# Scores of 32 left-over keys on four column tiles of the PE, spread by way of HBM, and the last chunk's sums behind its values

## The chip, the cores and the metric

One core of one Trainium2 chip. The metric is the device time of one execution in microseconds (us), median of several runs. PE is TensorE (its weight loads are shown as PEld), ACT is ScalarE, DVE is VectorE, POOL is GpSimd, SP is SyncE, which issues nearly all DMAs here.

## The reference, cut to what matters

```python
B, T, D = 2, 4000, 512
h = layernorm(x1)                                   # x1: after a first feed-forward block
q, k, v = h @ w_q, h @ w_k, h @ w_v
p = softmax(einsum('btd,bsd->bts', q, k) * D**-0.5)
x2 = x1 + einsum('bts,bsd->btd', p, v) @ w_o
# ... gated convolution with batch statistics, second feed-forward block, layernorm
```

Attention runs over 4000 keys for each of 2 x 4000 queries. Queries come in 16 chunks: 14 of 508 and 2 of 444 columns. 4000 keys are 31 tiles of 128 and 32 left over.

## The kernel before: the parts that matter

Weights are folded (`M` for queries and keys, `Wvo` for values and output), so keys and values are both `h`. For each key tile PE computes scores into a bank of PSUM, where its results land, ACT takes the exponential into a block `P`, DVE adds it to the running sums `acc`, and four steps later PE multiplies `P` with the keys' rows into four output banks.

```python
# attention, chunk g of W queries; KT = 32 key tiles, REST = 32, DC = 4, LAG = 4
for kt in range(KT):
    ps, b_ps = self.sbank()
    for cc in range(DC):                                # scores: 128 keys x W queries
        self.mm(ps[:, 0:W], self.hT[kc][:, kj, cc, :], self.qT[s][:, cc, 0:W], cc == 0, cc == DC - 1, ...)
    self.act(self.P[p][:, 0:W], ps[:, 0:W], AF.Exp, ...)
    n = REST if kt == KT - 1 else 128                   # of the last tile 32 rows count
    # DVE: acc[0:n] += P[0:n]
    if kt == KT - 1:
        self.split_sums(g)
    def values(...):                                    # four key tiles later
        for dc in range(DC):
            r = slice(dc*REST, (dc+1)*REST) if kt == KT - 1 else slice(0, 128)
            self.mm(self.Yb[dc][:, 0:W], self.h[kt][r, dc*128:(dc+1)*128], self.P[p][r, 0:W], ...,
                    **({"tile_position": (dc*REST, 0)} if kt == KT - 1 else {}))
```

The last key tile holds the same 32 keys four times, in rows 0-31, 32-63, 64-95 and 96-127. Its full-width scores are therefore four equal copies. The values use that: each of four row tiles of the PE takes one copy and makes a different quarter of the output, all at once. After the last chunk come the sums as matmuls of one column, then the last values:

```python
self.pop(3)                      # values of key tiles 28 to 30
self.sums_direct(last % 2)       # 8 matmuls with a column of ones, waits for split_sums
self.pop(1)                      # values of the left-over tile, then OT is copied out of PSUM
self.conv_b(tail, DC - 3)        # then the projections begin
```

## Time and profile before

| | before |
|---|---|
| time, median of 4 runs | 2040.98 us (2040.7 to 2041.0) |
| span of the profiled run | 2037.1 us |
| PE busy | 2028.9 us, 99% of the chain that ended last |
| one attention chunk of 508 queries | 68.32 us |
| scores of the left-over tile in it | 0.86 us |

How to read it: PE is full nearly throughout, so a change is worth what it takes off PE's stream, plus the few gaps at the seams between stages. Other engines only matter where they open such a gap.

### The profile page before, as it was taken

How to read it: one execution, taken by the hardware profiler on the slowest of the kernel's cores; microseconds unless marked ns; L12 is line 12 of the kernel's file. 1: busy time of each engine (PE TensorE's matmuls, PEld its weight loads, DVE VectorE, ACT ScalarE, POOL GpSimd, SP SyncE). 2: the span in 40 equal slices, each digit the busy share in tenths (PEclk: the TensorE clock that was granted, in tenths of full speed). 3: DMA queues.
4: the chain of work that ended last, by engine and by line, in shares of the span. 5: the costliest groups of instructions: out<-in, count | busy, mean ns of one | idle time of the engine just before them, and what ended most of it. 6: DMA issues, size and time to landing. Idle time of an engine off the chain costs nothing.

```text
span 2037.1 us, 24581 instructions
## 1 busy us (share of the span) xinstructions
PE 2028.9 (100%) x9682; PEld 1030.5 (51%) x9682; DVE 1081.5 (53%) x2187; ACT 743.7 (37%) x1277; POOL 107.6 (5%) x235
## 2 busy tenths in 40 slices
PE   9999999999999999999999999999999999999998
PEld 5555555554444444445444444444455555555555
DVE  4234443334556667666766676667674443434433
ACT  3433333333333333333333333333345443443433
POOL 1000000000000000000000000000011000000000
PEclk9999999999999999999999999999999999999999
DMA  8122245420101111114421111111143111111111
GB/s 189 49 62 62 54 102 124 96 70 19 16 16 27 25 32 26 27 26 94 106 57 23 26 29 32 24 27 26 44 135 93 32 32 42 32 32 42 29 34 38
DMA packets 253122, 104.43 MB, mean 51 GB/s; under 512 B 193412, under 2 KB 252487, under 8 KB 252999
## 3 DMA queue, kind: packets, MB, share of 16 engines
q1 hardware_dynamic: 252321, 102.44, 21.6%
q8 instruction: 78, 1.28, 0.3%
q14 instruction: 45, 0.37, 0.1%
q10 hardware_dynamic: 678, 0.34, 0.1%
HBM read 33.77 MB, written 23.34 MB: 28 GB/s over the span
## 4 chain that ended last, share of the span: by engine, by line
PE 99%; ACT 0%; DVE 0%; issue 0%; POOL 0%; DVEq 0%
PE s L512 56%; PE y L512 42%; ACT work L562 0%; DVE wff L1215 0%; PE y L540 0%; ACT keys L562 0%; POOL work L1224 0%; DVE work L559 0%; DVE work L876 0%; PE y L527 0%; DVE wff L1102 0%; DVE work L1222 0%; ACT xt L562 0%; DVE work L835 0%; DVE work L1229 0%
## 5 line engine op out<-in xcount | busy, mean ns | idle before, releaser
L562 ACT ACTIVATE work<-s 128x508 bf16<-128x508 f32 (+3 forms) x1060 | 621.7, 587 | 1211.5 <-PE s L512 1207.1
L512 PE MATMUL s<-work,wff 128*128 128x508 bf16 (+4 forms) x2640 | 628.3, 369 | 0.8 <-ACT work L562 0.4
L512 PE MATMUL s<-work,keys 128*128 128x508 bf16 (+1 forms) x2048 | 516.6, 374 | 0.1
L512 PE MATMUL y<-work,keys 128*128 128x508 bf16 (+2 forms) x2048 | 503.9, 373 | 0.0
L512 PE MATMUL y<-wff,work 128*127 128x512 bf16 (+1 forms) x2000 | 501.4, 378 | 0.0
L959 DVE TENSOR_TENSOR work<-work 128x508 f32<-128x508 f32 (+2 forms) x496 | 334.4, 674 | 281.6 <-ACT work L562 280.8
L512 PEld LDWEIGHTS s<-work,wff 128*128 128x128 bf16 x2640 | 252.6, 98 | 277.0 <-issue 4.7
L512 PEld LDWEIGHTS y<-wff,work 128*127 128x127 bf16 x2000 | 274.4, 137 | 170.9
L512 PEld LDWEIGHTS s<-work,keys 128*128 128x128 bf16 x2048 | 199.4, 98 | 232.0 <-DVE work L876 0.6
L512 PEld LDWEIGHTS y<-work,keys 128*128 128x128 bf16 (+1 forms) x2048 | 193.6, 97 | 233.1 <-issue 6.2
L758 DVE SCALAR_TENSOR_TENSOR xt<-y,xt 127x512 bf16<-127x512 f32 x125 | 77.7, 682 | 364.0 <-PE y L512 364.0
L512 PE MATMUL s<-work 128*127 128x512 bf16 (+4 forms) x775 | 196.9, 378 | 1.2 <-DVE work L1333 1.2
L624 DVE BATCH_NORM_STATS2 work<-xt 127x6 f32<-127x512 bf16 x311 | 195.2, 676 | 5.2 <-DMA xt<-in_x_dram 4.9
L631 POOL TENSOR_TENSOR work<-work 127x4 f32<-127x4 f32 (+1 forms) x76 | 76.5, 1007 | 1129.4 <-DVE work L629 1129.4
L512 PEld LDWEIGHTS s<-work 128*127 128x127 bf16 (+2 forms) x775 | 94.8, 124 | 75.6 <-issue 4.0
L644 DVE TENSOR_SCALAR work<-xt,work 127x512 bf16<-127x512 bf16 x309 | 111.4, 406 | 27.4 <-POOL work L631 23.2
L758 DVE SCALAR_TENSOR_TENSOR xt<-s,xt 127x512 bf16<-127x512 f32 x55 | 38.0, 691 | 148.7 <-PE s L512 148.7
L758 DVE SCALAR_TENSOR_TENSOR xt<-s,work,xt 127x512 bf16<-127x512 f32 x64 | 48.0, 750 | 30.9 <-PE s L512 30.3
L1113 DVE SCALAR_TENSOR_TENSOR wff<-wff,s 128x508 bf16<-128x508 f32 (+1 forms) x57 | 38.7, 678 | 41.5 <-PE s L512 41.3
L562 ACT ACTIVATE wff<-s 128x508 f32<-128x508 f32 (+1 forms) x67 | 39.5, 591 | 53.5 <-PE s L512 53.4
L562 ACT ACTIVATE work<-keys,work 128x508 bf16<-128x508 bf16 (+1 forms) x68 | 52.3, 774 | 0.4 <-DVE work L1229 0.2
L1194 POOL COPY wff<-wff 128x1 bf16<-128x1 bf16 x56 | 10.4, 187 | 637.8 <-DVE wff L1113 635.0
(92 smaller groups left out, 413.0 us busy)
## 6 DMA issues: line engine op xcount, KB each, us to landing
keys<-keysd SPq DMA_DIRECT2D x62, 128.0 KB, 2.3
keysd<-work SPq DMA_DIRECT2D x14, 448.0 KB, 3.2
out_dram<-work SPq DMA_DIRECT2D x14, 448.0 KB, 3.2
dcvd<-wff SPq DMA_DIRECT2D x48, 127.0 KB, 1.9
keys<-dcvd SPq DMA_DIRECT2D x12, 508.0 KB, 4.9
xt<-in_x_dram SPq DMA_DIRECT2D x13, 448.0 KB, 4.8
wff<-in_w_ff_a_dram SPq DMA_DIRECT2D x15, 256.0 KB, 5.2
work<-work SPq DMA_TRANSPOSE x208, 2.5
```

Source lines behind the costliest of these rows:

```text
L512: self.S.op("PE", lambda e: e.matmul(out, lhsT, rhs, start=start, stop=stop, **kw), reads=reads, writes=[bank], inc=stop if inc is None el ...
L562: return self.S.op("ACT", lambda e: e.activation(out, in_, func, **kw), reads=reads, writes=writes)
L624: self.S.op("DVE", lambda e: e.bn_stats(self.st[sl][:, ti, 0:6], x), reads=[b_x], writes=[self.b_st[sl][ti]])
L631: S.op("POOL", lambda e: e.tensor_tensor(out=self.rs[sl][:, 0:n], in0=self.mv[sl][:, 0:n, 1], in1=self.neghalf[0:TILE, 0:n], op=ALU.pow), ...
L644: self.S.op("DVE", lambda e: e.tensor_scalar(out, x, self.mv[sl][:, ti, 0:1], self.rs[sl][:, ti:ti + 1], ALU.subtract, ALU.mult), reads=[b ...
L758: self.S.op("DVE", lambda e: e.scalar_tensor_tensor(out=self.XT[g][rows], in0=ps[rows], scalar=scalar, in1=self.XT[g][rows], op0=ALU.mult, ...
L959: S.op("DVE", lambda e, p=p, n=n, acc=acc: e.tensor_tensor(out=acc, in0=acc, in1=self.P[p][0:n, 0:W], op=ALU.add), reads=[self.b_P[p], sel ...
L1113: self.S.op("DVE", lambda e: e.scalar_tensor_tensor(out=out, in0=th, scalar=1.0, in1=ps[:, 0:W], op0=ALU.add, op1=ALU.mult), reads=[b_ps, ...
L1194: S.op("POOL", lambda e: e.tensor_copy(self.G[gs][:, jj, 0:1], self.G[gp][:, jj, CHUNK:CHUNK + 1]), reads=[self.b_G[gp][jj]], writes=[self ...
```

## The change

Its intent: the scores of the 32 left-over keys are computed once and not four times. The 128 columns of the PE become four column tiles of 32; tile j holds the 32 keys and gets the j-th quarter of the queries, so 127 columns stream and not 508. The result then lies by quarters of the queries (rows 32j to 32j+31 hold quarter j), while the values want all queries in each of the four row groups. A store to HBM and four loads spread it. This happens at key tile 18, long before the values need it. Three smaller parts: at the start of attention matmuls of the feed-forward block move behind the last query group; in the last chunk the sums go behind the left-over values, with a block of the convolution behind the first projection; two PSUM copies go from ACT to DVE.

```diff
+    TAIL_AT = 18
+        self.pq = W.view(14336, 128); self.ptail = W.view(31744, CHUNK); self.pqd = nc.dram_tensor("pqd", [128, TILE], ...)
...
             for kt in range(KT):
+                if kt == self.TAIL_AT:
+                    self.tail_scores(g)
+                if kt < KT - 1:
                     (scores, exponential and sums of one key tile, as before)
...
-                        self.mm(self.Yb[dc][:, 0:W], self.h[kt][r, ...], self.P[p][r, 0:W], ...
+                        (the last tile reads self.ptail in place of self.P[p])
...
+    def tail_scores(self, g):
+        n = W // 4
+        parts = [(slice(j * REST, (j + 1) * REST), slice(j * n, (j + 1) * n)) for j in range(4)]
+        for cc in range(DC):
+            for j, (r, q) in enumerate(parts):
+                self.mm(ps[r, 0:n], hT[:, cc, r], self.qT[s][:, cc, q], cc == 0, cc == DC - 1, ...,
+                        inc=cc == DC - 1 and j == 3, tile_position=(0, j * REST))
+        self.act(self.pq[:, 0:n], ps[:, 0:n], AF.Exp, ...)
+        for r, q in parts:
+            (DVE: acc[s][r, q] += pq[r, 0:n])
+        self.store(self.pqd[:, 0:n], self.pq[:, 0:n], ...)
+        src = self.pqd[:, 0:n].rearrange("(j k) q -> k j q", j=4)
+        S.dma("SP", k, *[lambda e, r=r: e.dma_start(self.ptail[r, 0:W]..., src) for r, q in parts], ...)
...
         for dc in range(DC):
-            if dc == DC - 1:
-                self.pop(1)
             self.q_group(0, 0, dc)
+        self.pop(1)
...
         self.pop(3)
+        self.pop(1)
         self.sums_direct(last % 2)
-        self.pop(1)
-        self.conv_b(tail, DC - 3)
-        fill = [None, ...
+        fill = [lambda: self.conv_b(tail, DC - 3), ...
...
-        copy_away()
+        copy_away("DVE")
```

Left out: the load of the second batch's left-over keys moves from the 25th key tile of the second batch's first chunk to its 7th, since they are now needed at key tile 18.

More of the change, by code (lines that the diff above doesn't have):

```diff
@@ L359, in memory @@
         self.b_Wp2 = C.buf("Wp2", oWvo, 4096)
+        self.pq = W.view(14336, 128)
+        self.b_pq = W.buf("pq", 14336, 256)
+        self.ptail = W.view(31744, CHUNK)
+        self.b_ptail = W.buf("ptail", 31744, 2 * CHUNK)
+        self.pqd = nc.dram_tensor("pqd", [128, TILE], BF16, kind="Internal").ap()
+        self.b_pqd = Buf("pqd")
         GW = CHUNK + 4
@@ L942, in attention @@
                 kc, kj = divmod(kt, TPC)
-                ps, b_ps = self.sbank()
-                p = self.nxt("Pa", self.NP - 1) if self.any_score else self.nxt("P", self.NP)
-                for cc in range(DC):
-                    self.mm(ps[:, 0:W], self.hT[kc][:, kj, cc, :], self.qT[s][:, cc, 0:W],
-                            cc == 0, cc == DC - 1 and not self.any_score,
-                            [self.b_hT[kc][kj], self.b_qT[s][cc]], b_ps)
-                if self.any_score:
-                    self.mm(ps[:, 0:W], self.one3, self.m3[:, 0:W], False, True,
-                            [self.b_one3] + self.b_m3, b_ps)
@@ L952, in attention @@
-                self.act(self.P[p][:, 0:W], ps[:, 0:W], AF.Exp, [b_ps], [self.b_P[p]], scale=SCALE)
-                if kt == 0:
-                    S.op("DVE", lambda e, p=p: e.tensor_copy(self.acc[s][:, 0:W], self.P[p][:, 0:W]),
-                         reads=[self.b_P[p]], writes=[self.b_acc[s]])
-                else:
-                    n = REST if kt == KT - 1 else 128
-                    acc = self.acc[s][0:n, 0:W]
-                    S.op("DVE", lambda e, p=p, n=n, acc=acc: e.tensor_tensor(
-                        out=acc, in0=acc, in1=self.P[p][0:n, 0:W], op=ALU.add),
-                        reads=[self.b_P[p], self.b_acc[s]], writes=[self.b_acc[s]])
+                p = None
@@ new lines, in attention @@
+                if kt == self.TAIL_AT:
+                    self.tail_scores(g)
+                if kt < KT - 1:
+                    ps, b_ps = self.sbank()
+                    p = self.nxt("Pa", self.NP - 1) if self.any_score else self.nxt("P", self.NP)
+                    for cc in range(DC):
+                        self.mm(ps[:, 0:W], self.hT[kc][:, kj, cc, :], self.qT[s][:, cc, 0:W],
+                                cc == 0, cc == DC - 1 and not self.any_score,
+                                [self.b_hT[kc][kj], self.b_qT[s][cc]], b_ps)
+                    if self.any_score:
+                        self.mm(ps[:, 0:W], self.one3, self.m3[:, 0:W], False, True,
+                                [self.b_one3] + self.b_m3, b_ps)
+                    self.act(self.P[p][:, 0:W], ps[:, 0:W], AF.Exp, [b_ps], [self.b_P[p]], scale=SCALE)
+                    acc = self.acc[s][:, 0:W]
+                    if kt == 0:
+                        S.op("DVE", lambda e, p=p: e.tensor_copy(acc, self.P[p][:, 0:W]),
+                             reads=[self.b_P[p]], writes=[self.b_acc[s]])
+                    else:
+                        S.op("DVE", lambda e, p=p: e.tensor_tensor(out=acc, in0=acc, in1=self.P[p][:, 0:W], op=ALU.add),
+                             reads=[self.b_P[p], self.b_acc[s]], writes=[self.b_acc[s]])
@@ L969, in values @@
                     for dc in range(DC):
-                        r = slice(dc * REST, (dc + 1) * REST) if kt == KT - 1 else slice(0, 128)
-                        self.mm(self.Yb[dc][:, 0:W], self.h[kt][r, dc * 128:(dc + 1) * 128], self.P[p][r, 0:W],
-                                kt == 0, kt == KT - 1, [self.b_h[kt], self.b_P[p]], self.b_Y[dc],
-                                inc=kt == KT - 1 or dc == DC - 1,
-                                **({"tile_position": (dc * REST, 0)} if kt == KT - 1 else {}))
+                        r, x, b_x, at = slice(0, 128), self.P[p or 0], self.b_P[p or 0], {}
+                        if kt == KT - 1:
+                            r, x, b_x, at = slice(dc * REST, (dc + 1) * REST), self.ptail, self.b_ptail, {"tile_position": (dc * REST, 0)}
+                        self.mm(self.Yb[dc][:, 0:W], self.h[kt][r, dc * 128:(dc + 1) * 128], x[r, 0:W],
+                                kt == 0, kt == KT - 1, [self.b_h[kt], b_x], self.b_Y[dc],
+                                inc=kt == KT - 1 or dc == DC - 1, **at)
                     if kt == KT - 1:
@@ L994, in attention @@
                     for k in range(KT):
-                        if 6 + k * (2 * KT - 12) // KT == at:
+                        if (6 + k * (2 * KT - 12) // KT if k < KT - 1 else KT + 6) == at:
                             self.key_tile(1, k)
@@ L998, in attention @@
                 self.tick()
+    def tail_scores(self, g):
+        S, s, W = self.S, g % 2, width(g)
+        n = W // 4
+        ps, b_ps = self.sbank()
+        hT, b_hT = self.hT[TCB - 1][:, TPC - 1], self.b_hT[TCB - 1][TPC - 1]
+        parts = [(slice(j * REST, (j + 1) * REST), slice(j * n, (j + 1) * n)) for j in range(4)]
+        for cc in range(DC):
+            for j, (r, q) in enumerate(parts):
+                self.mm(ps[r, 0:n], hT[:, cc, r], self.qT[s][:, cc, q], cc == 0, cc == DC - 1 and not self.any_score,
+                        [b_hT, self.b_qT[s][cc]], b_ps, inc=cc == DC - 1 and j == 3, tile_position=(0, j * REST))
+        if self.any_score:
+            for j, (r, q) in enumerate(parts):
+                self.mm(ps[r, 0:n], self.one3[:, r], self.m3[:, q], False, True, [self.b_one3] + self.b_m3, b_ps,
+                        inc=j == 3, tile_position=(0, j * REST))
+        self.act(self.pq[:, 0:n], ps[:, 0:n], AF.Exp, [b_ps], [self.b_pq], scale=SCALE)
+        for r, q in parts:
+            acc = self.acc[s][r, q]
+            S.op("DVE", lambda e, acc=acc, r=r: e.tensor_tensor(out=acc, in0=acc, in1=self.pq[r, 0:n], op=ALU.add),
+                 reads=[self.b_pq, self.b_acc[s]], writes=[self.b_acc[s]])
+        self.store(self.pqd[:, 0:n], self.pq[:, 0:n], [self.b_pq], [self.b_pqd])
+        k = S.dsems[self.nxt("ld", 16)]
+        src = self.pqd[:, 0:n].rearrange("(j k) q -> k j q", j=4)
+        S.dma("SP", k, *[lambda e, r=r: e.dma_start(self.ptail[r, 0:W].rearrange("p (j q) -> p j q", j=4), src)
+                         for r, q in parts], reads=[self.b_pqd], writes=[self.b_ptail])
     def key_tile(self, b, kt):
@@ L1216, in depthwise @@
                                   reads=[b_ps], writes=[self.b_bst[cc]]),
-                lambda: self.act(self.dcv[t][cc][:, 0:W], ps[:, 0:W], AF.Copy, [b_ps], [self.b_dcv[t][cc]]))
+                lambda eng="ACT": self.away(eng, self.dcv[t][cc][:, 0:W], ps[:, 0:W], b_ps, [self.b_dcv[t][cc]]))
     def conv_scale(self, cc):
@@ L1404, in program @@
         for dc in range(DC):
-            if dc == DC - 1:
-                self.pop(1)
-                old -= 1
             self.q_group(0, 0, dc)
+        self.pop(1)
+        old -= 1
         tail = NCK - 2
@@ L1457, in gate @@
             gates.pop(0)(eng)
-        fill = [None, lambda: gates.append(self.conv_a(tail, DC - 3)), lambda: self.conv_b(tail, DC - 2),
+        fill = [lambda: self.conv_b(tail, DC - 3), lambda: gates.append(self.conv_a(tail, DC - 3)), lambda: self.conv_b(tail, DC - 2),
                 lambda: gates.append(self.conv_a(tail, DC - 2))]
@@ L1465, in prepare @@
                 gate("POOL")
-            if fill[ti]:
-                fill[ti]()
+            fill[ti]()
         for ti in self.ln_tiles(last, self.nxt("ln", self.LN_SLOTS), prepare, ("ACT", "ACT", "DVE", "DVE")):
@@ L1494, in finish, with copy_away @@
             self.conv_scale(cc)
-        def copy_away():
+        def copy_away(eng="ACT"):
             while copies:
-                copies.pop(0)()
+                copies.pop(0)(eng)
         self.halo_left(last, 0)
```

## The prediction

> **What bounds the kernel now.** I read the page's busy row first, then the chain that ended last, then what PE waited for, then the groups by form, and last the timeline of PE around the instructions that the diff touches.
>
> ```profile
> PE 2028.9 (100%) x9682; PEld 1030.5 (51%) x9682; DVE 1081.5 (53%) x2187; ACT 743.7 (37%) x1277; POOL 107.6 (5%) x235
> PE 99%; ACT 0%; DVE 0%; issue 0%; POOL 0%; DVEq 0%
> ```
>
> The first line is busy time, share of the span and instructions; the second is the chain of waits by engine. PE is busy 2028.9 of 2037.1 us and carries 99% of the chain. A busy PE need not be a full one, so I asked what it waited for:
>
> ```profile
> PE s L512 <- DVE work L1333: 1.2, 1, 1.2
> PE s L512 <- ACT work L562: 0.4, 1, 0.4
> ```
>
> Columns: the wait in all, how often, the longest. These are its two longest waits, 1.6 us together. So only two things can move the time: fewer PE columns, or the handful of gaps at the seams between stages. Time taken off DVE, ACT or the DMA is worth nothing here.
>
> Now the step that the diff replaces. 4000 keys are 31 tiles of 128 and 32 left over, and the leftovers stand four times in a 128-key tile. Each of the 16 query chunks pays full-width scores for them:
>
> ```profile
> 715.44 1.02 PE L512 MATMUL y<-work,keys 128*128 128x508 bf16 x4
> 716.29 1.02 PE L512 MATMUL s<-work,keys 128*128 128x508 bf16 x4
> 717.25 0.39 PE L512 MATMUL y<-work,keys 32*128 32x508 bf16 x4
> 717.58 0.61 PE L512 MATMUL s<-work,wff 128*128 128x508 bf16 x2
> ```
>
> Columns: start, length, and what ran. Starts matter, since matmuls overlap. A full group of four goes from 715.44 to 716.29: 0.85 to 0.86 us, 0.215 a matmul. The line at 716.29 is the leftover scores; the one at 717.25 is the leftover values, already packed as four row tiles. That pack starts 0.96 us after the scores rather than 0.86, so a change of tiling costs 0.10 us on entering. The four then take as long as one (0.39 for all, and the group's mean of one is 383 ns), and the next full-width matmul starts 0.33 us later, against the 0.215 of one matmul: 0.11 us on leaving. This is the best witness for the new pack: four tiles at the price of one, and 0.21 us of switching.
>
> ```profile
> L512 PE MATMUL y<-work,keys 32*128 32x508 bf16 x56 | 5.5, 383 | 0.0
> L512 PEld LDWEIGHTS y<-work,keys 32*128 32x128 bf16 x64 | 1.6, 90 | 6.2 <-issue 6.2
> L959 DVE TENSOR_TENSOR work<-work 128x508 f32<-128x508 f32 x420 | 287.0, 683 | 256.7 <-ACT work L562 256.4
> L959 DVE TENSOR_TENSOR work<-work 128x444 f32<-128x444 f32 x60 | 36.9, 615 | 21.9 <-ACT work L562 21.4
> L959 DVE TENSOR_TENSOR work<-work 32x508 f32<-32x508 f32 x14 | 9.2, 661 | 2.1 <-ACT work L562 2.1
> ```
>
> Here the 6.2 us that the weight loads of the 16 row packs sat idle, 0.39 each, says the same as the timeline: no weights are loaded ahead across a switch.
>
> **What the Trainium skill says.** "TensorEngine Tiling (Array Packing)", section Key Properties: a change of tiling mode drains the TensorE, while tiles of one mode load weights and multiply in parallel. The trace agrees: the 0.10 and 0.11 above. "TensorE: Matmul & The Clock Gate", Part 3, section Measured speedup vs the span model: a pack should last one matmul plus about 4 ns for each further tile, and three column tiles with 512 columns measured 2.38x. The trace agrees for row tiles (0.39 against 0.383); it holds no column tile. The same page, section The mechanism, says weight loads overlap matmuls in flight only when the row group differs. The four column tiles share all row groups, so this warns that they may not overlap as the row tiles do; no line here can tell. "DMA: Bandwidth & Descriptors", section Specifications: transfers under 512 B are slow. The new ones move rows of 127 x 2 = 254 B. The page's 193412 of 253122 packets are that small already, and it shows 1.9 us to landing for a store of this kind and 2.3 for a load of keys.
>
> **The change, part by part.**
>
> 1. Removed: 16 groups of leftover scores. 14 chunks x 0.86 + 2 short chunks (444 queries) x 0.75 = 13.5 us of PE. The 0.75 is the step of the 444-column groups in the last chunk's timeline (1488.36 to 1489.11).
>
> 2. Added: per chunk 16 matmuls of 127 columns on 32x128 weights, four column tiles in each of four rounds. For the price of 127 columns I take the 16 matmuls of this size in the first LayerNorm chunk:
>
> ```profile
> 8.57 1.06 PE L512 MATMUL s<-work,wff 128*128 128x127 bf16 x16
> 9.47 0.39 PE L527 MATMUL y<-work 127*128 127x127 bf16 x4
> ```
>
> 16 from 8.57 to 9.47 is 0.056 us each, with full weight loads behind them. If four tiles go as one, a pack is 4 x 0.056 + 0.21 = 0.43 us. If they go one by one, it is 16 x 0.056 + 0.21 = 1.11 us, more than the 0.86 it replaces. I expect overlap, but not perfect: each round needs new weights in the same four column groups, and I allow 0.03 us a round for that (my estimate). That makes 0.55 us, and about 0.52 for the 111 columns of a short chunk. Gain: 14 x (0.86 - 0.55) + 2 x (0.75 - 0.52) = 4.3 + 0.5 = 4.8 us.
>
> 3. The values of the leftovers stay a row pack; only their source changes. No change.
>
> 4. DVE: one add of 32x508 (661 ns) becomes four of 32x127. The slope between the 508 and 444 forms is (683 - 615) / 64 = 1.06 ns a column, so 127 columns are about 280 ns and four are 1.1 us: 0.45 us more a chunk, 7 us in all on an engine busy half the time. ACT loses a little. Neither is on the path.
>
> 5. DMA: one store and four loads a chunk through HBM. By the order of the changed program they stand behind four transposes of the LayerNorm on the sync queue. In a middle chunk these run from 749.77 to 754.89. Then store 1.9, about 1.6 for issuing four loads, 2.3 to land: ready near 761. The leftover values follow at 785.57, so there is 24 us of slack.
>
> 6. The start of attention. The last two query groups fed PE without filler, and this wait followed:
>
> ```profile
> 453.68 2.19 PE L512 MATMUL s<-work,keys 128*128 128x508 bf16 x8
> 455.71 0.81 PE L512 MATMUL y<-wff,work 128*127 128x512 bf16 x3
> ```
>
> 8 matmuls took 2.03 us to the next group instead of 1.72: 0.3 us, the copy of the last query group on DVE. Moving four FF matmuls behind that group covers it: -0.3.
>
> 7. The end of attention. Before, the sums (8 matmuls of one column) wait for DVE's split, and the leftover values stand behind them:
>
> ```profile
> 1513.65 0.74 PE L512 MATMUL s<-work 128*127 128x1 bf16 x8
> 1514.32 0.37 PE L512 MATMUL y<-work,keys 32*128 32x444 bf16 x4
> 1514.62 1.04 PE L512 MATMUL s<-work,wff 128*128 128x508 bf16 x4
> ```
>
> Now the values go first and the sums run while the output is copied out of PSUM. The wait of 0.2 us in the sums goes; but the block that used to hide the copies moves behind the first projection, which may give 0.1 back. Two copies of about 0.55 us leave ACT for DVE at the Silu stage, where ACT carries 4.13 us of the chain from 1542.16: perhaps -0.4. I put the end at -0.6.
>
> Sum: -4.8 - 0.3 - 0.6 = -5.7 us; 2040.97 - 5.7 = 2035.3 us, a ratio of 0.9972.
>
> **The rivals.**
>
> Column tiles in series. For it: the skill's remark on row groups, and that each round waits for new weights. Against: the measured 2.38x for three. It makes +0.25 us a chunk, about +4 us, so 2040.97 + 4 - 0.9 = 2044.
>
> Perfect overlap, 0.43 us a pack: 14 x 0.43 + 2 x 0.35 = 6.7 us, so 2040.97 - 6.7 - 0.9 = 2033.4.
>
> The trip through HBM becomes the wait. Were the spread keys late by 1 to 2 us in each chunk, the time would be 2050 to 2065. The 24 us of slack speak against it; only a sync queue blocked for long in the last chunk, where it fetches convolution tiles, could do it, and there once.
>
> DVE falls behind at the LayerNorm of the same stretch, four adds beside casts and normalizations. Its adds in 749 to 757 had 0.2 to 1.9 us of idle time before them, so a delay is absorbed: at most 1 us in all.
>
> **Range and chances.** The pack's price is nearly all of the uncertainty: 0.43 gives 2033.4, 0.55 gives 2035.3, 0.8 gives 2039.2. I hold overlap to be likely, at about 85%, and the seams uncertain by 1 us either way. So 2032.4 to 2040.0 for 8 in 10. Two per cent is 41 us; the removed work is 13.5 us, so faster by that much is excluded but for an accident: 0.003. Slower by 41 us needs a wait of 2.5 us in every chunk: 0.012. Within 2%: 0.985.
>
> **What would show it right or wrong.** In the changed profile the column pack should start about 0.96 us after the full group ahead of it and the next full group about 0.45 us after the pack's start (0.33 if the overlap is perfect, 1.0 in series: this one number tells the rivals apart). The chunk's period, 68.32 us from 717.25 to 785.57, should be 68.0. No wait of PE on the spread keys' DMA should appear, and PE should still carry 99% of the chain. The wait at the start of attention should be gone. I am wrong if the pack takes over 0.86 us, if PE waits for that DMA, or if the gain comes from the seams rather than from the 16 packs.

## The result, and the profile after

| | before | changed |
|---|---|---|
| time, median of 4 runs | 2040.98 us (2040.7 to 2041.0) | 2034.34 us (2033.42 to 2034.57) |
| ratio | | 0.9967 (0.9950 to 0.9984) |
| span of the profiled run | 2037.1 us | 2030.5 us |
| PE busy | 2028.9 us | 2021.3 us |

Ratios are the mean time of one kernel's fast runs over that of the other's of the same rounds, so not quite the ratio of the medians. The change is 6.6 us faster by the medians, 0.3%; 5.7 us were predicted.

The page of the changed kernel, busy time and the chain by engine, then the two longest of PE's waits below the 1.2 us at the program's start that both kernels have:

```profile
PE 2021.3 (100%) x9874; PEld 1026.5 (51%) x9874; DVE 1089.1 (54%) x2237; ACT 740.0 (36%) x1275; POOL 108.0 (5%) x235
PE 99%; DVE 0%; ACT 0%; DMA 0%; issue 0%; POOL 0%; DVEq 0%; ACTq 0%
```

```profile
PE y L536 <- DVE work L653: 0.9, 1, 0.9
PE s L521 <- DMA work<-work: 0.7, 1, 0.7
```

PE still carries everything. One wait is new in kind: PE for a DMA, `work<-work`, the transposes of LayerNorm output, and not for the spread keys. The other is in the first 12 us of the program, which the change does not touch.

The pack itself, in the timeline of PE in the same chunk as shown of before (start, length, what):

```profile
747.13 1.02 PE L521 MATMUL y<-work,keys 128*128 128x508 bf16 x4
748.08 1.38 PE L521 MATMUL s<-work,keys 128*32 128x127 bf16 x20
749.29 1.02 PE L521 MATMUL y<-work,keys 128*128 128x508 bf16 x4
```

The view merges the 16 small matmuls with the four full ones that follow, since they read and write the same tensors. Starts tell them apart: the pack begins 0.95 us after a full group of 0.86, so it cost 0.09 to enter; 1.21 us pass to the next values, of which 0.86 are the four full scores, so 0.35 from the pack's start to the first full matmul. Entry and pack are 0.44 us in the place of 0.86.

The groups by form, and what SP's queue did in that chunk:

```profile
L1031 DVE TENSOR_TENSOR work<-work,wff 32x127 f32<-32x127 f32 x56 | 15.7, 280 | 1.7 <-ACT wff L571 0.2
L521 PE MATMUL s<-work,keys 128*32 128x127 bf16 x224 | 5.7, 222 | 0.0
L521 PEld LDWEIGHTS s<-work,keys 128*32 128x32 bf16 x256 | 3.7, 96 | 6.6 <-ACT work L571 5.8 <-issue 0.8
```

```profile
747.51 5.92 SPq L579 DMA_TRANSPOSE work<-work  x4
753.47 0.58 SPq L588 DMA_DIRECT2D pqd<-wff  x1
755.22 1.74 SPq L1036 DMA_DIRECT2D wff<-pqd  x4
```

224 small matmuls, 14 packs, kept PE busy for 5.7 us: 0.41 a pack with the drain at its end. The four small adds on DVE took 280 ns each. The loads were issued by 756.96; the page has 1.8 us to landing for them, so the spread keys lay ready near 759 for values that come at 782.89.

To see where the 6.6 us are, I compared the start of the same matmul in both profiles, stage by stage:

| start of | before | changed | difference |
|---|---|---|---|
| the first scores of attention | 453.68 | 453.38 | -0.30 |
| the left-over values of chunk 0 | 515.71 | 514.68 | -1.03 |
| the left-over values of chunk 14 | 1460.12 | 1453.38 | -6.74 |
| the second feed-forward block | 1548.44 | 1541.45 | -6.99 |
| end of the span | 2037.1 | 2030.5 | -6.6 |

The first row is chance: both kernels give PE the same work until then, and the ten experiments below have this point between 453.38 and 454.07. So is the last: from the start of PE's last matmul, 5.3 to 6.3 us pass until the end of the span, in whichever kernel. Between chunk 0 and chunk 14 every chunk gains 0.41 us (0.34 in the short one). From there to the second feed-forward block lie the pack of the last chunk, 0.34, and the reordered stages; together they gain 0.25 only, so something was given back. It is this, in the last chunk, the pair of convolution blocks at key tile 22; before and changed:

```profile
1495.11 0.91 PE L512 MATMUL y<-work,keys 128*128 128x444 bf16 x4
1496.17 1.67 PE L512 MATMUL s<-work,wff 128*128 128x508 bf16 x7
```

```profile
1488.79 0.91 PE L521 MATMUL y<-work,keys 128*128 128x444 bf16 x4
1490.40 0.81 PE L521 MATMUL s<-work,wff 128*128 128x508 bf16 x3 [0.69 <-DMA work<-work]
```

Four matmuls of 444 columns take 0.75 us to the next start. Before, 1.06 passed, a gap of 0.31 that I had not noticed; changed, 1.61, a gap of 0.86. The 0.55 between them is what was given back.

### The profile page after: what moved, and what is told of

Its sections match the earlier page's. It is cut to its first block, busy times and chain, and to the rows that moved or that the text cites. A ratio compares the mean times of both kernels' runs of the same rounds, so it can differ in the third digit from the quotient of the medians.

```text
span 2030.5 us, 25096 instructions
## 1 busy us (share of the span) xinstructions
PE 2021.3 (100%) x9874; PEld 1026.5 (51%) x9874; DVE 1089.1 (54%) x2237; ACT 740.0 (36%) x1275; POOL 108.0 (5%) x235
## 4 chain that ended last, share of the span: by engine, by line
PE 99%; DVE 0%; ACT 0%; DMA 0%; issue 0%; POOL 0%; DVEq 0%; ACTq 0%
PE s L521 56%; PE y L521 43%; DVE work L633 0%; DMA work<-work 0%; ACT work L571 0%; PE y L549 0%; POOL work L740 0%; PE y L536 0%; DVE work L1376 0%; DVE work L735 0%; DVE work L653 0%; DVE work L568 0%; DVE wff L1254 0%; ACT keys L571 0%; DVE wff L1141 0%
## 5 line engine op out<-in xcount | busy, mean ns | idle before, releaser
L571 ACT ACTIVATE work<-s 128x508 bf16<-128x508 f32 (+3 forms) x1044 | 613.8, 589 | 1197.8 <-PE s L521 1192.4
L521 PE MATMUL s<-work,keys 128*128 128x508 bf16 (+2 forms) x2240 | 505.8, 356 | 0.0
L521 PE MATMUL y<-work,keys 128*128 128x508 bf16 (+1 forms) x1984 | 495.1, 373 | 0.0
L971 DVE TENSOR_TENSOR work<-work 128x508 f32<-128x508 f32 (+1 forms) x480 | 324.3, 676 | 265.2 <-ACT work L571 262.5
L521 PEld LDWEIGHTS s<-work,keys 128*128 128x128 bf16 (+1 forms) x2240 | 195.7, 97 | 228.9 <-ACT work L571 5.8
L521 PEld LDWEIGHTS y<-work,keys 128*128 128x128 bf16 x1984 | 192.1, 97 | 226.7 <-DVE work L568 0.5
L571 ACT ACTIVATE wff<-s 128x508 f32<-128x508 f32 (+2 forms) x83 | 44.0, 531 | 64.2 <-PE s L521 64.1
```

Source lines behind the costliest of these rows:

```text
L521: self.S.op("PE", lambda e: e.matmul(out, lhsT, rhs, start=start, stop=stop, **kw), reads=reads, writes=[bank], inc=stop if inc is None el ...
L571: return self.S.op("ACT", lambda e: e.activation(out, in_, func, **kw), reads=reads, writes=writes)
L971: S.op("DVE", lambda e, p=p: e.tensor_tensor(out=acc, in0=acc, in1=self.P[p][:, 0:W], op=ALU.add), reads=[self.b_P[p], self.b_acc[s]], wri ...
```

## The experiments

All ten runs gave correct results (the tenth is the changed kernel again). Each has 4 or 5 executions beside the kernel before on one chip; times are medians, with the kernel before at 2041.35 (first four), 2041.06 (next four) and 2040.64 us (last two).

### The packs alone, and everything else alone

```diff
 # packs alone: the kernel before with tail_scores, ptail and the earlier key load; none of the other edits
 # seams alone: the changed kernel's query groups, sums and copies, with left-over scores at full width at key tile 31
```

> The kernel before with the column packs and their trip through HBM alone; start of attention, last chunk's sums and Silu copies as before. If the packs are the whole gain: 14 x 0.42 + 2 x 0.34 = 6.6 us, about 2034.4, less what the last chunk's wait for its transposed LayerNorm output takes (0.3 us in the profile before, 0.86 in the changed one). If the seams were worth the 0.9 us of the prediction, this run must be 0.9 us slower than the changed kernel.

Measured: 2035.59 us, 5.8 below before (ratio 0.9972). It had the gap in the last chunk, 1.08 us.

> The other half: leftover scores at full width as before, with the moved query groups, the sums behind the values and the two copies on VectorE. Prediction: 0.9 us faster than before (2040.1). Rival, by the changed profile, where the gaps after the sums and in the Silu stage stand at the same size: only the 0.3 us at the start of attention, 2040.7 or no visible difference.

Measured: 2040.41 us, 0.9 below before; the ratio 0.9996 (0.9982 to 1.0009) does not separate it from before by time alone. The trace does: PE's stream is shorter by 0.3 at the start of attention, as these lines of the packs alone and of the seams alone show (8 full matmuls to the next group: 2.03 against 1.72 us),

```profile
453.58 2.19 PE L521 MATMUL s<-work,keys 128*128 128x508 bf16 x8
455.61 0.59 PE L521 MATMUL y<-wff,work 128*127 128x512 bf16 x2
```

```profile
454.04 1.88 PE L512 MATMUL s<-work,keys 128*128 128x508 bf16 x8
455.76 0.81 PE L512 MATMUL y<-wff,work 128*127 128x512 bf16 x3
```

and by 0.4 in the Silu stage (9.95 us from 1538.49 to the second feed-forward block before, 9.55 with the seams alone). There the 16 transposes on PE no longer wait for ACT; before and seams alone:

```profile
1546.35 1.10 PE L540 MATMUL y<-work 127*128 127x127 bf16 x12 [0.25 <-ACT work L562]
```

```profile
1545.45 1.65 PE L540 MATMUL y<-work 127*128 127x127 bf16 x16
```

By the last projection the sums had gained less than 0.1. So the packs are 5.8 by the medians and the seams 0.8 by the trace (0.3 + 0.4 + under 0.1), together the change's 6.6. My rival for the seams, that only the 0.3 would be seen, is wrong; it misread the changed profile, where PE has no wait for ACT in the Silu stage.

### The order of the small matmuls

```diff
-        for cc in range(DC):
-            for j, (r, q) in enumerate(parts):
+        for j, (r, q) in enumerate(parts):
+            for cc in range(DC):
```

> The changed kernel, with the 16 small matmuls in another order: the four weight blocks of one column tile in a row, then the next tile. Same work, same switches. If the saving is the overlap of different column tiles, neighbours now share a tile and must follow each other: 16 x 0.056 + 0.21 = 1.1 us a pack against 0.44, so 16 x 0.67 = 10.6 us slower than the changed kernel, about 2045. If the hardware sorts it out (each tile has its own stream), nothing changes.

Measured: 2034.49 us, the changed kernel's time. Its pack in the timeline:

```profile
747.29 1.02 PE L521 MATMUL y<-work,keys 128*128 128x508 bf16 x4
748.24 1.41 PE L521 MATMUL s<-work,keys 128*32 128x127 bf16 x20
749.49 1.02 PE L521 MATMUL y<-work,keys 128*128 128x508 bf16 x4
```

0.95 to enter and 1.25 to the next values: 0.48 by the same arithmetic, 0.04 more than in the changed kernel (0.03 by the chunk's period, 67.94 against 67.91). Over 16 packs that is 0.5 us; the total is equal because this run's gap in the last chunk was 0.34 and not 0.86. My theory said 0.67 more a pack. Two explanations were left: a column tile takes several matmuls at once, or PE starts a later tile's matmul while an earlier tile's next one still waits. The next run tells them apart.

### Sixteen more on one tile, and the pack twice

```diff
 # after the pack's own 16, on the first tile only (same scores again, the result stays right)
+        for m in range(4):
+            r, q = parts[0]
+            for cc in range(DC):
+                self.mm(ps[r, 0:n], hT[:, cc, r], self.qT[s][:, cc, q], cc == 0, ..., tile_position=(0, 0))
 # control: the pack's own 16 issued a second time, over the four tiles
-        for cc in range(DC):
+        for rep, cc in [(m, c) for m in range(2) for c in range(DC)]:
```

> The changed kernel with 16 more of the small matmuls behind each pack, all on the first column tile (the first quarter's scores four times over, so the result stays right). The run in the order column by column cost only 0.03 us a pack, so either theory is open. If a column tile takes one matmul at a time, these 16 cost 16 x 0.055 = 0.88 us a pack, 14 us in all (2048). If what counts is only how many small matmuls are in flight, whatever the tile, they cost 16 x 0.014 = 0.22 us a pack, 3.6 us in all (2038).

> The changed kernel with each pack's 16 matmuls issued twice, in the changed kernel's order over the four tiles. The control for the run on one tile, and the pack's own cost without its switches: 4 rounds x 0.055 = 0.22 us more a pack, 3.5 us in all (about 2037.9). If switching were paid inside the pack too, more.

Measured: 2047.33 us with 16 more on one tile and 2037.47 us with the pack twice. Their packs, in this order:

```profile
752.27 2.26 PE L521 MATMUL s<-work,keys 128*32 128x127 bf16 x36
754.37 0.80 PE L521 MATMUL y<-work,keys 128*128 128x508 bf16 x3
```

```profile
749.40 1.60 PE L521 MATMUL s<-work,keys 128*32 128x127 bf16 x36
750.85 1.02 PE L521 MATMUL y<-work,keys 128*128 128x508 bf16 x4
```

From the pack's start to the values after it: 2.10 and 1.45 us, against 1.21 in the changed kernel. So 16 more on one tile are 0.89 us, 0.056 each: one tile takes one matmul at a time. 16 more over four tiles are 0.24, or 0.06 a round: four tiles run as one. Both agree with the 0.056 us that a 127-column matmul of full width takes. The control also splits the pack: 0.24 us stream, and the other 0.2 of its 0.44 are the two changes of tiling.

With this the run in column order has one explanation left. In program order, one at a time on a tile, the fourth tile's first matmul could not start before nine waits of 0.056 us, and the 16 would take 12 waits, 0.67 us, before the last one streams. They took 0.04 more than in the changed order. The starts say the same: here is the column order's pack again, with the view cut off at 748.29.

```profile
748.24 0.27 PE L521 MATMUL s<-work,keys 128*32 128x127 bf16 x4
```

Four matmuls had started within 0.05 us, where one tile alone took one every 0.056. So PE does not start matmuls of different column tiles strictly in program order; it lets a later tile's pass one that waits for its own tile. (The trace gives each record's start but not its tile, so this is inferred from the totals and the starts.)

### The pack late, to test the slack of the trip through HBM

```diff
-    TAIL_AT = 18
+    TAIL_AT = 30
```

> The pack at key tile 30 instead of 18, so the store and the loads have some 6 key-tile steps (9 to 10 us) instead of 24 us. They need about 7 us if nothing stands before them on the sync queue. Slack theory: no difference to the changed kernel within 0.5 us. Rival (the trip becomes a wait): PE waits for the loads at the leftover values of every chunk, visible as PE waiting for the DMA of the spread keys.

Measured: 2034.12 us, the same as the changed kernel. In the middle chunks no wait appeared: the store was issued at 774.63, the loads between 776.12 and 777.86, and the values came at 782.90. PE waited for the spread keys once, in the last chunk:

```profile
PE y L521 <- DMA wff<-pqd: 0.5, 1, 0.5
```

There no next chunk lies between: the pack ran at 1501.77, the store left at 1502.49 and the loads were issued until 1505.76, while PE was through with all earlier values near 1506.8. So the trip takes 5 to 6 us when nothing stands before it on the queue. At key tile 18 its slack is 24 us; at key tile 30 it is 3 us in a middle chunk, still free, and less than nothing in the last. That the total is nevertheless the same has a reason in the last chunk: in this run its four transposes took 5.14 us, as before the change, and PE's gap at them was 0.32 and not 0.86, which pays for the 0.5.

### Row pack and column pack side by side

A change of tiling costs 0.09 to 0.11 us, and the changed kernel has four in each chunk. In 14 of 16 chunks the new pack can stand directly behind the row pack of the chunk before:

```diff
-                if kt == self.TAIL_AT:
+                if kt == self.TAIL_AT and qc == 0:
                     self.tail_scores(g)
...
                 elif len(self.lags) > LAG:
                     self.pop(1)
+                if kt == LAG - 1 and qc:
+                    self.tail_scores(g)
```

> The changed kernel, but the column pack of a chunk follows at once on the row pack of the chunk before (key tile 3), in 14 of 16 chunks. If a change of tiling costs 0.10 us each time it leaves or enters full width, and row to column is one change, a pair of packs has three changes instead of four: 14 x 0.10 = 1.4 us faster than the changed kernel, about 2032.9. If row to column drains no more than tile to tile, two changes instead of four, 2.8 us.

Measured: 2032.81 us (ratio to before 0.9962), with these packs:

```profile
713.93 1.02 PE L521 MATMUL s<-work,keys 128*128 128x508 bf16 x4
714.88 0.39 PE L521 MATMUL y<-wff,keys 32*128 32x508 bf16 x4
715.21 0.41 PE L521 MATMUL s<-work,keys 128*32 128x127 bf16 x16
715.55 1.90 PE L521 MATMUL s<-work,wff 128*128 128x508 bf16 x8
```

Entering the row pack: 0.95 after a group of 0.86, 0.09 more. Row to column: 0.33, where 508 columns stream in 0.21 to 0.22, so again 0.1. Column to full: 0.34 from the pack's start, as in the changed kernel. Three changes, not four: the first of the two theories. It should be 1.4 us; between chunk 1 and chunk 14 each chunk is indeed 0.1 us shorter than in the changed kernel. The gap in the last chunk is here too, 1.08 us.

### The wait in the last chunk

```diff
 # the hook of attention; tail is chunk 14, the last one whose convolution starts inside attention
-            if kt in (22, 27) and (0 <= g - 1 < tail or g - 1 == tail and (22, 27).index(kt) < self.KEEP):
+            if kt in (22, 27) and 0 <= g - 1 < tail:
                 pair(g - 1, (22, 27).index(kt))
+            if kt == 23 and g - 1 == tail:
+                pair(g - 1, 0)
```

> The same, and in the last chunk the convolution pair starts at key tile 23 instead of 22, behind the transposes that PE waited for (0.31 us in the kernel before, 0.86 in the changed one, 1.09 in the packs alone, where one of the four transposes was issued over 2 us long). The wait should be gone: 0.3 to 0.9 us below the adjacent packs, about 2032.3.

Measured: 2031.99 us (ratio to before 0.9956, 0.9942 to 0.9969), 0.8 below the adjacent packs in the same call. It is the fastest kernel of this study: 9.1 us below before in its call, where the change is 6.6 below in its own.

> The changed kernel with only the last chunk's convolution pair one key tile later, packs apart as in the change. If the wait for the transposes is worth what the profiles show, 0.3 us when no transpose is slow and 0.9 to 1.1 when one is, this is 0.3 to 0.9 us faster than the changed kernel in the same call, and its gap in the last chunk is gone from the trace.

> The changed kernel itself once more, as the reference for the run beside it and for the spread between profiles: about 2034.3. If the slow transpose falls on the same instruction of the same program again, the gap of 0.86 us in the last chunk stands again; if it falls at random (about one transpose in twelve in attention), it is more likely 0.3.

Measured: 2033.34 us with the later pair and 2034.51 us for the changed kernel again. Two of the five runs with the later pair were slower (2034.71 and 2035.02), so that the ratios to before, 0.9967 and 0.9968, do not separate the two; the traces do. The changed kernel again, then the later pair:

```profile
1482.83 6.31 SPq L579 DMA_TRANSPOSE work<-work  x4
1490.62 0.59 PE L521 MATMUL s<-work,wff 128*128 128x508 bf16 x2 [0.91 <-DMA work<-work]
```

```profile
1482.84 5.98 SPq L579 DMA_TRANSPOSE work<-work  x4
1491.06 1.24 PE L521 MATMUL s<-work,wff 128*128 128x508 bf16 x5
```

The four transposes start at the same time in both, and in both take more than the 5.15 us that they took before. In the changed kernel PE stands at them; one key tile later, they have landed. By PE's last matmul the later pair is 1.05 us ahead.

Why do they take longer? Most transposes hold SP's queue for 1.19 to 1.27 us, but 8 to 16 of the 178 in attention, by profile, hold it for 1.4 to 2.9. Which one is not random: in the two profiles of the changed kernel (12 and 11 slow ones) 10 are the same instructions. For the last chunk's four, the traces show (us):

| | the four on the queue | from their start until PE has no other work | PE's gap |
|---|---|---|---|
| before, and seams alone | 5.15 | 6.29, 6.30 | 0.31 |
| pack late | 5.14 | 6.29 | 0.32 |
| column order | 5.61 | 6.74 | 0.34 |
| pack twice | 5.55 | 6.91 | 0.11 |
| sixteen more on one tile | 5.82 | 7.49 | none |
| changed kernel | 6.09 | 6.71 | 0.86 |
| changed kernel again | 6.31 | 6.71 | 1.08 |
| packs alone | 6.33 | 6.72 | 1.08 |
| adjacent packs | 5.91 | 6.30 | 1.08 |
| later pair, packs apart | 5.98 | 8.22 | none |
| later pair, packs adjacent | 5.92 | 7.79 | none |

The gap is the first number less the second plus 1.46, within 0.02 us, and there is none where this comes out below zero. So PE waits here for these four, in the kernel before too. The column pack, where it stands in this stretch, gives them 0.4 us more time; a slow transpose takes 0.4 to 1.2 us more than the others.

The five DMAs more in each chunk seem to shift which instruction is hit: with the pack at key tile 30 none of these four is slow, with it at key tile 18 or 3 one is in every profile. What makes a transpose slow stays open; no run here tells.

## Why the prediction was right

Right in the time (2035.3 against 2034.34) and in what bounds the kernel. By its own steps:

1. Removed scores, 13.5 us of PE: as told, 0.86 a chunk.
2. The pack: this term was mis-sized. I allowed 0.03 us a round for weights that would not load behind the matmuls, 0.55 us a pack; it measured 0.44, in a short chunk 0.41. The rounds follow each other at 0.06 us, so the weight loads lie wholly behind the matmuls, and my rival of perfect overlap (0.43) had the size. That is 14 x 0.41 + 2 x 0.34 = 6.4 us (0.41 and 0.34 as the chunks' periods shrank) where 4.8 stood. The trace of before could have told: the 16 full-width matmuls that I took the 0.056 us from change the weights of the same row and column groups each time, and nothing is added for it. Of the signs that I named, the pack's start came after 0.95 us (0.96 told), the next full group 0.35 after it (0.45 told, 0.33 for perfect overlap), and the chunk's period is 67.91 (68.0 told). The rival of tiles in series is refuted: one tile in series is 0.056 a matmul, and the pack would have cost 1.1.
3. The values unchanged: their row pack took 0.39 before and after.
4. DVE: 280 ns an add, as estimated, and off the path.
5. The trip through HBM: ready near 759, 761 told. No wait; with the pack 12 key tiles later one showed, in the last chunk alone. The rows of 254 B landed in 1.7 us (store) and 1.8 us (load); no run moves the same bytes in longer rows, so whether the warning that I cited on transfers under 512 B bears on them is not shown.
6. The start of attention: 0.3 told, 0.3 measured. (The matmuls that moved are three, not the four that I told.)
7. The end: 0.6 told, about 0.5 measured (0.4 in the Silu stage and under 0.1 from the sums, where 0.4 and 0.2 stood).

Not foreseen: the last chunk's wait for its transposes, which took back 0.55 us. I had named the sync queue of the last chunk as a danger, but for the spread keys; it was the LayerNorm's transposes, ahead of the new DMAs in the queue, that were late. The sum of what the profiles show, 6.4 + 0.3 + 0.5 - 0.55 = 6.65, stands beside a measured 6.6; the tenths of chance at the program's two ends cancel in the two profiles (-0.30 and +0.38). The mis-sized pack (1.6 us more gain than told) and the unforeseen wait (0.55 less) had opposite signs, so the total came out better than its terms, and that was luck.

## What to carry to other kernels

When PE is full, a tile of few keys or rows is worth packing by columns, but price it by its two changes of tiling as well as by its stream: here they are half of the pack. Put packs side by side to share a change, and fetch rearranged results through HBM only where many microseconds lie between. After any shortening of the bound engine, look for a wait that was short and is now longer: here such a wait took back half a microsecond, and starting one block of work one key tile later removed it.

## What the Trainium skill lacked or had wrong

- "TensorE: Matmul & The Clock Gate", Part 3, section The mechanism, has matmuls in strict order in start and end. For column tiles the runs contradict it: 16 matmuls in column-by-column order took 0.48 us with their tiling changes, where 16 on a single tile took 0.89 without, so later tiles' matmuls must have passed waiting ones; four of the 16 had started within 0.05 us.
- The same section's list has weight loads overlap matmuls in flight only for another row group (the text before it also allows a background weight buffer). The four column tiles share all row groups, and the rounds still follow at 0.06 us, a 127-column matmul's own cadence: nothing is added for their weights. Nor is it for full-width matmuls, 0.056 us each with new weights every time.
- The same page's measured speedups for column tiles alone end at three tiles, 2.38x at 512 columns. Sixteen matmuls of 127 columns took 0.24 us on four tiles and 0.89 on one: 3.7x in a full stream, tiling changes apart.
- "TensorEngine Tiling (Array Packing)", section Key Properties, says that a change of mode drains the PE but not what it costs: 0.09 to 0.11 us each, measured for full to row, row to full, full to column, column to full and row to column, the last being one change.
- No page has it: most DMA transposes of this kernel hold SP's queue for 1.19 to 1.27 us, but 8 to 16 of the 178 in attention hold it for 1.4 to 2.9, and in two profiles of one program 10 of them were the same instructions.
